# Pooled attention with expert routing: eleven unread TensorE products under the first loads, eighteen more behind the first bound sums and among the first maxima, and new places for the first three pairs

## The chip, the core and the metric

The kernel runs on one core of a Trainium2 chip. The core has TensorE (matmul), VectorE, ScalarE, GpSimd and SyncE (which issues most DMAs); each works through its own list of instructions in order and waits on semaphores for the others. The metric is the device time of one execution, in microseconds, as the median of several runs. Lower is better.

## The reference

The kernel computes attention with pooled queries, and then an expert layer with a fixed capacity on its output. Cut to what matters:

```python
def _attn_ref(q, k, v):                      # each (8, 8, 1152, 64)
    q_pool = q.reshape(B, H, S // 2, 2, D).mean(axis=3)
    scores = 1 / np.sqrt(D) * np.matmul(q_pool, k.transpose(0, 1, 3, 2))
    scores = scores - np.max(scores, axis=-1, keepdims=True)
    attn = np.exp(scores)
    attn = attn / (np.sum(attn, axis=-1, keepdims=True) + 1e-09)
    return np.matmul(attn, v)

def _moe_ref(x, w_gate, w1, w2):             # 4608 tokens, 8 experts, 576 each
    logits = x @ w_gate
    ...                                      # tokens to experts, best logit first, 576 per expert
    for e in range(E):
        out[mask_e] = np.maximum(x[mask_e] @ w1[e], 0) @ w2[e]
```

The change touches only the attention part, and there only how it begins.

## The kernel before, in words

Attention works on 32 pairs of heads. A pair takes 18 steps, nine blocks of 128 keys for each of its two heads `s`. A step is: scores on TensorE (`qk`, line 776, into `sc0` or `sc1`), the exponential on ScalarE (line 779, into `P`), the low half of the weights on GpSimd or VectorE (`PM`, line 783), and five steps later the weighted sums on TensorE (line 793, into `av0` or `av1`). Operands are split into a high and a low 16-bit half (`KH` and `KL`, `QH` and `QL`), so each score is a sum of products of 128 and of 65 or 69 rows.

Before a pair's steps come its preparations:

- Loads by SyncE: `QD` or `QS` (queries), `KD` (keys, two halves), `VD` (values), and `WB`, a piece of an expert's weights.
- Bounds (`bounds`, lines 520 to 581): ScalarE sums absolute values and squares into `VM` and `VQ`, TensorE adds them over the partitions into `mb` (tag `vs`, lines 537 to 545), VectorE takes the exponent bits into `VE` (lines 553, 555, 558), ScalarE makes the scales `SC` and `EX` (lines 564 to 573), VectorE the limit (line 576).
- Splits (`split`, `values`): `KH`, `QH`, scaled `KD` and `QS`, then `KL`, `QL`, and the two halves of the values in `V`. For the first two pairs GpSimd makes the low halves, later VectorE.
- `spread`: SyncE copies these halves to the tiles from which the scores are made (`KA`, `KB`, `QA`, `QB`).
- Row maxima (`max_chunk`): TensorE makes products of `QH` and `KH` and VectorE reduces each to a maximum. For pair 0 these are 15 chunks for head 0 (tags `mm0`, `mr0`) and 15 for head 1 (`mm1`, `mr1`), each a product of 64 rows by 384 columns (line 684, maxima at line 687); the chunks of head 0 use the five banks `ma`, `av0`, `sc0`, `av1`, `sc1`. For later pairs there are 18 chunks of 512 columns and three of the ends (lines 693 and 703, maxima at 696 and 705). A fold (line 724), a transpose into `mb` (line 738) and, for pair 0, two instructions with `ndiag` (lines 742 and 745) put the maxima into rows of `QB`; the scores of a head need them.

Pair 0's maxima, its splits and its copies therefore stand before the first score.

The order of all this is set ahead of time. `Cycle.plan` puts the items into a list by a number from a table: for an item of tag `x` the number is the table's entry plus 25 times its pair, and the smallest number whose inputs are already in the list comes next. Pairs 0, 1 and 2 have tables of their own, `TAU0`, `TAU1` and `TAU2`; all others use `TAU`. Each engine then runs its items in the list's order; waits on the chip follow from the tiles that they read and write.

Unread products (tags `wu`, `wv`, `wx`, line 916) multiply a tile of ones with a tile of ones, 128 rows by 512 columns, into `av0` or `av1`; nothing reads the result. There are 10 of tag `wu` and 13 of tag `wx`. The table puts five of them at the start, five behind pair 0's first bound sums, and 13 between the chunks of the maxima.

## Time and profile before

| | |
|---|---|
| median of 3 runs | 1232.99 us |
| lowest and highest | 1231.44 and 1235.9 us |
| profiled execution | 1237.53 us, of which its span 1235.8 us |
| TensorE busy | 1190.0 us, 96% of the span |
| VectorE, ScalarE, GpSimd busy | 82%, 79%, 73% |

The profile is of one execution, and all later rows are of it. A timeline row gives the start, the length and the engine of an instruction or of several alike, the line in the program, and in brackets how long the engine stood idle before it and what released it. A row of the chain of waits is one piece of the path that ended last. A row of the windows view gives the busy time of each engine in a stretch.

### The profile page before, as it was taken

The numbers are of one execution on the slowest core, as the hardware profiler recorded it, in microseconds if no ns is written. First come the engines' busy times: TensorE is split into PE (matmuls) and PEld (weight loads), VectorE is DVE, ScalarE is ACT, GpSimd is POOL, SyncE is SP. The second block draws the span as 40 slices with busy tenths as digits, with TensorE's granted clock in tenths as the row PEclk, the third lists the DMA queues.
The fourth block names the chain that finished last, engine by engine and source line by source line (L and its number), as shares of the span: only waits on it lengthen the run. The fifth ranks groups of instructions, "written<-read, shape, count | busy, mean of one in ns | idle before, by whom it ended". The sixth has DMA issues, their size and how long they took to land.

```text
span 1235.8 us, 38902 instructions
## 1 busy us (share of the span) xinstructions
PE 1190.0 (96%) x15470; PEld 860.7 (70%) x15470; DVE 1018.7 (82%) x2743; ACT 972.0 (79%) x1719; POOL 901.6 (73%) x879
## 2 busy tenths in 40 slices
PE   7899999999999999999999999789999999999998
PEld 2567778778778777777787788465657466575673
DVE  6899899999999999999999995779888898893520
ACT  6979899999899898999999986065876686786751
POOL 6978898898888998888888887044775584675641
PEclk9999999999999999999999999889999999999999
DMA  8666776876776866776876730042453554547401
GB/s 250 151 158 165 186 189 163 196 186 160 191 185 160 193 182 162 195 184 159 197 188 157 180 93 20 20 175 86 129 196 111 159 192 130 171 138 230 120 31 39
DMA packets 131218, 190.83 MB, mean 154 GB/s; under 512 B 50268, under 2 KB 86108, under 8 KB 128732
## 3 DMA queue, kind: packets, MB, share of 16 engines
q1 hardware_dynamic: 117948, 126.75, 38.9%
q0 software_dynamic: 12944, 61.58, 17.5%
q8 instruction: 121, 1.98, 0.7%
q14 instruction: 61, 0.50, 0.1%
q10 hardware_dynamic: 144, 0.02, 0.0%
HBM read 116.41 MB, written 18.87 MB: 109 GB/s over the span
## 4 chain that ended last, share of the span: by engine, by line
PE 77%; DVE 13%; DMA 4%; issue 2%; ACT 2%; POOL 0%; SPq 0%; POOLq 0%; ACTq 0%; DVEq 0%
PE sc L776 20%; PE av L793 18%; PE ph L1561 11%; PE po L1591 11%; PE mb L693 4%; PE ma L693 4%; DVE MX L696 3%; PE av L828 1%; DMA BD<-QH 1%; PE av L840 1%; ACT P L779 1%; DMA W<-in_w_dram,widx 1%; PE po L1597 1%; PE rt L1194 1%; DVE HX L1570 1%
## 5 line engine op out<-in xcount | busy, mean ns | idle before, releaser
L783 POOL TENSOR_TENSOR PM<-P 128x576 f16<-128x576 f32 x508 | 612.4, 1266 | 99.6 <-ACT P L779 48.3
L779 ACT ACTIVATE P<-sc,EX 128x576 f32<-128x576 f32 x576 | 412.6, 739 | 76.0 <-PE sc L776 58.8
L793 PEld LDWEIGHTS <-P 128*128 128x128 bf16 x5760 | 293.0, 98 | 30.0 <-issue 1.9
L793 PE MATMUL av<-V,P 128*128 128x65 f16 (+1 forms) x5760 | 301.2, 192 | 0.0
L793 PE MATMUL av<-V,PM 128*128 128x65 f16 x2880 | 292.8, 194 | 0.0
L793 PEld LDWEIGHTS <-PM 128*128 128x128 f16 x2880 | 263.8, 97 | 0.0
L776 PE MATMUL sc<-QA,KA 128*128 128x288 f16 x1152 | 234.5, 285 | 1.4 <-ACT P L779 1.3
L776 PE MATMUL sc<-QB,KB 65*128 65x288 f16 (+1 forms) x1152 | 235.7, 285 | 0.0
L696 DVE TENSOR_REDUCE MX<-mb 128x1 f32<-128x512 f32 x279 | 190.7, 684 | 27.8 <-PE mb L693 22.7
L696 DVE TENSOR_REDUCE MX<-ma 128x1 f32<-128x512 f32 x279 | 190.6, 683 | 9.8 <-PE ma L693 6.8
L776 PEld LDWEIGHTS <-KA 128*128 128x128 f16 x1152 | 106.2, 97 | 73.1 <-issue 22.7
L1591 PE MATMUL po<-W2H,HX 128*128 128x512 f16 x512 | 155.5, 379 | 0.0
L1561 PE MATMUL ph<-XH,W1H 128*128 128x320 f16 (+1 forms) x512 | 146.2, 286 | 0.7 <-DVE WE L1539 0.3
L1561 PE MATMUL ph<-XL,W1H 128*128 128x320 f16 (+1 forms) x512 | 146.2, 286 | 0.6 <-DVE XL L1455 0.6
L1561 PE MATMUL ph<-XH,W1L 128*128 128x320 f16 (+1 forms) x512 | 145.9, 286 | 0.0
L776 PEld LDWEIGHTS <-KB 65*128 65x128 f16 (+1 forms) x1152 | 112.5, 98 | 29.4
L1591 PEld LDWEIGHTS <-HX 128*128 128x128 f16 x768 | 71.2, 98 | 78.5 <-issue 0.5
L1561 PEld LDWEIGHTS <-W1H 128*128 128x128 f16 x1024 | 97.9, 98 | 30.7 <-issue 6.1
L1613 POOL DMA_INDIRECT out_dram<-OT,idx x40 | 39.2, 980 | 109.1 <-ACT OT L1593 91.2
L693 PE MATMUL ma<-KH,BD 128*128 128x512 f16 x279 | 105.7, 379 | 3.5 <-DVE MX L696 1.3
L693 PE MATMUL mb<-KH,BD 128*128 128x512 f16 x279 | 105.5, 378 | 3.3 <-DVE MX L696 1.4
L1514 POOL TENSOR_TENSOR W2L<-W,W2H 128x512 f16<-128x512 f32 x64 | 73.2, 1159 | 38.5 <-ACT W L1512 34.1
(308 smaller groups left out, 2157.9 us busy)
## 6 DMA issues: line engine op xcount, KB each, us to landing
KD<-in_kt_dram SPq DMA_DIRECT2D x64, 288.0 KB
VD<-in_v_dram SPq DMA_DIRECT2D x32, 576.0 KB
WB<-in_w_dram SPq DMA_DIRECT2D x32, 512.0 KB
QA<-QH SPq DMA_DIRECT2D x128, 72.0 KB
KB<-KH SPq DMA_DIRECT2D x64, 144.0 KB
KA<-KH SPq DMA_DIRECT2D x64, 144.0 KB
KA<-KL SPq DMA_DIRECT2D x64, 144.0 KB
x_dram<-X SPq DMA_DIRECT2D x16, 576.0 KB
```

Source lines behind the costliest of these rows:

```text
L693: od.add(t, "PE", 214, lambda: nc.tensor.matmul(m, BD[i][:, j, :], KH[i][:, 512 * c:512 * c + 512], start=True, stop=True), r=bd + [("KH", ...
L696: od.add(t, "DVE", 597, lambda: nc.vector.tensor_reduce(MX[i][:, j, c:c + 1], m, axis=AX.X, op=OP.max), r=[mk], w=[("MX", i, j, c)], tag=" ...
L776: nc.tensor.matmul(c[:, t, :288], a[i][:rows, s, ks], b[i][:rows, s, 288 * t:288 * t + 288], start=first, stop=not first)
L779: od.add(g + 0.1, "ACT", 624, lambda: nc.scalar.activation(p.rearrange("p (t q) -> p t q", t=2), c[:, :, :288], AF.Exp, scale=EX[n % 3][:, ...
L783: od.add(g + 0.2, en, dur, lock=1, fn=lambda: eng.tensor_tensor(pm, p, hi, op=OP.subtract), r=[("P32", g % NP)], w=[("PM", g % NM)], tag="pm")
L793: nc.tensor.matmul(out, w[:, qs], v, start=kb == 0 and j == 0 and y == 0, stop=kb == NKB - 1 and y == 2, skip_group_check=True)
L828: nc.tensor.transpose(m[:, 128 * z:128 * z + 128], X[u][:, 3 * q + z], ident)
L840: nc.tensor.matmul(av[1][32 * q:32 * q + E, :384], wgs[:, c], XT[q].rearrange("p c t -> p (c t)"), start=True, stop=True)
L1514: od.add(tt, "POOL", 1230, lambda o=lo[p], a=raw[p], h=hi[p]: nc.gpsimd.tensor_tensor(o, a, h, op=OP.subtract), r=[key, hk, sk], w=[(nm + ...
L1561: nc.tensor.matmul(p, a[:, d, fs], b[:, d, qs], start=z == 0, stop=z == 11)
L1591: nc.tensor.matmul(o, a[:, z, q0:q0 + 128], b[:, z], start=z == 0 and y == 0, stop=z == 7 and y == 2)
L1613: st = nc.gpsimd.indirect_dma_start(out=out, out_offset=bass.IndirectOffsetOnAxis(ap=idx[i][:n, c:c + 1], axis=0), in_=OT[ob][:n], in_offs ...
```

## The change

Three things are done.

1. Tables: eleven unread products (`wu`) now stand at the very start, and the 13 of tag `wx` are gone.
2. In `bounds`, for pair 0, a new item of tag `wv` runs six unread products into `av1` behind the first bound sums. In `max_chunk`, each chunk of head 0 but three is followed by one unread product into the second half of `sc0`. That makes 11 + 6 + 12 = 29 unread products where there were 23.
3. `TAU0`, `TAU1` and `TAU2` get new numbers throughout; `TAU`, and with it the order of the other 29 pairs within themselves, stays.

```diff
-... "wu": [-17.875, -17.555, -17.235, -16.915, -16.595, -16.275, -15.955, -15.635, -15.315, -14.995], "wx": [...]
+... "wu": [-300, -299.99, -299.98, -299.97, -299.96, -299.95, -299.94, -299.93, -299.92, -299.91, -299.9], "wv": [-250],
...
-      5, "np": 10, "nm": 10, "stick": 1, "nx": 3, "wu": 10, "pd": [4, 12], "wv": 0, "pd0": [], "pd1": [1, 2, 4, 9, 10,
-      15, 16, 17], "d1": 2.0, "cw1": 0.7, "wx": 13, "wy": 0}
+      5, "np": 10, "nm": 10, "stick": 1, "nx": 3, "wu": 11, "pd": [4, 12], "wv": 0, "pd0": [], "pd1": [1, 2, 4, 9, 10,
+      15, 16, 17], "d1": 2.0, "cw1": 0.7, "wx": 0, "wy": 0}
...
         od.add(t + AT["bs"], "DVE", 250 if not a else 190, bits, r=["mb"], w=[("VE", i, c) for c in range(a, b)], tag="vs")
+        if not n and not a:
+            def busy():
+                for _ in range(6):
+                    nc.tensor.matmul(av[1], ones, wide, start=True, stop=True)
+            od.add(t + AT["bs"], "PE", 1280, busy, r=["mb"], w=["av1"], tag="wv")
...
-            od.add(t, "PE", 163, lambda: nc.tensor.matmul(
-                m[:q, :384], QH[i][r, 128 * j:128 * j + q], KH[i][r, 384 * c:384 * c + 384], start=True, stop=True),
-                r=[("QH", i)] + [("KH", i, z) for z in ((0,), (0, 1), (1,))[c]], w=[mk], tag="mm" + "01"[h])
+
+            def chunk():
+                nc.tensor.matmul(m[:q, :384], QH[i][r, 128 * j:128 * j + q], KH[i][r, 384 * c:384 * c + 384], start=True, stop=True)
+                if not h and (j, c) not in ((0, 2), (2, 1), (2, 2)):
+                    nc.tensor.matmul(sc[0][:, 1], ones, wide, start=True, stop=True)
+
+            od.add(t, "PE", 163 if h else 376, chunk, r=[("QH", i)] + [("KH", i, z) for z in ((0,), (0, 1), (1,))[c]], w=[mk], tag="mm" + "01"[h])
```

How the lists move at the places that matter here. First TensorE, from pair 0's bound sums to the first products of the maxima (`down` and `VM` are of the bound sums, `ones` and `wide` of the unread products, `sc_166` is `sc0`, `av_169` is `av1`). Before:

```order
L542 MATMUL mb<-VM_126,down 128x2 [waits Activation_49]
L916 LDWEIGHTS ones
L916 MATMUL av_169<-wide,ones 128x512
...
L684 LDWEIGHTS QH_89 [waits DVE_49]
L684 MATMUL av_169<-KH_85,QH_89 128x384 [waits Activation_49]
L684 LDWEIGHTS QH_89
L684 MATMUL sc_166<-KH_85,QH_89 128x384
```

and after:

```order
L541 MATMUL mb<-VM_126,down 128x2 [waits Activation_49]
L565 LDWEIGHTS ones
L565 MATMUL av_169<-wide,ones 128x512
...
L690 LDWEIGHTS QH_89 [waits DVE_49]
L690 MATMUL sc_166<-KH_85,QH_89 128x384 [waits Activation_49]
L692 LDWEIGHTS ones
L692 MATMUL sc_166<-wide,ones 128x512
L690 LDWEIGHTS QH_89
L690 MATMUL av_169<-KH_85,QH_89 128x384
L692 LDWEIGHTS ones
L692 MATMUL sc_166<-wide,ones 128x512 [waits DVE_49]
```

Five unread products (now six) precede the first chunk in both; behind each chunk now stands one into `sc0`, and the second of these waits for VectorE, for the maximum that reads `sc0`'s first half (two more of the twelve wait in the same way).

Second ScalarE, from pair 0's scales to its splits (`SC_113`, `EX_116` are the scales, `VJ,VQ<-VD` is the square over the values). Before:

```order
L564 ACTIVATE SC_113<-VE_135 128x2
L572 ACTIVATE EX_116<-SC_113 128x1
L573 ACTIVATE EX_116<-VE_135 128x1
L595 ACTIVATE KH_85<-KD_119,SC_113 128x576
L600 ACTIVATE QS_124<-QS_124,SC_113 128x576
L595 ACTIVATE KH_85<-KD_119,SC_113 128x576
L598 ACTIVATE KD_119<-KD_119,SC_113 128x576
L532 ACTIVATE VJ,VQ<-VD_122 128x1152
```

and after:

```order
L568 ACTIVATE SC_113<-VE_135 128x2
L599 ACTIVATE KH_85<-KD_119,SC_113 128x576
L576 ACTIVATE EX_116<-SC_113 128x1
L577 ACTIVATE EX_116<-VE_135 128x1
L604 ACTIVATE QS_124<-QS_124,SC_113 128x576
L531 ACTIVATE VJ,VQ<-VD_122 128x1152
L599 ACTIVATE KH_85<-KD_119,SC_113 128x576
L602 ACTIVATE KD_119<-KD_119,SC_113 128x576 x2
```

KH's first half moves ahead of both EX, its second half behind the square over VD.

Third VectorE, where `ndiag` is built. Before, among the last maxima of head 0:

```order
L687 TENSOR_REDUCE MX_137<-ma 128x1
L687 TENSOR_REDUCE MX_137<-sc_166 128x1
L493 TENSOR_SCALAR ndiag<-scratch 128x640 [waits Pool_49]
L687 TENSOR_REDUCE MX_137<-sc_166 128x1 [waits PE_49]
L687 TENSOR_REDUCE MX_137<-ma 128x1
L724 TENSOR_REDUCE CM_106<-MX_137 128x4 [waits DVE_49]
```

and after, ahead of the first work on a loaded tile:

```order
L394 MEMSET floor 128x3
L395 MEMSET floor 128x1
L492 TENSOR_SCALAR ndiag<-scratch 128x640 [waits Pool_49]
L592 TENSOR_TENSOR QS_124<-QD_121 128x576 [waits DMAHW1_49]
L500 MEMSET P_140 128x64
```

It leaves the list of the maxima and stands under the first loads.

## Rows read from the trace of the kernel before

**Rows 1.** Windows: stretch, length, busy us of PE, PEld, DVE, ACT, POOL, then PEclk.

```profile
24.40:55.76 31.36, 28.22 (x393) 18.53 (x393) 24.75 (x55) 27.98 (x49) 28.90 (x25) 1.00 0.52 139
...
55.76:79.30 23.54, 20.38 (x265) 13.99 (x263) 21.47 (x43) 17.52 (x31) 17.35 (x19) 1.00 0.63 149
...
125.00:725.00 600.00, 597.70 (x9944) 474.56 (x9942) 554.21 (x1095) 550.24 (x954) 525.07 (x467) 1.00 0.71 177
```

**Rows 2.** Chain of waits: start us, length us, what.

```profile
38.50 4.35 DVE MX L696 x7
...
69.26 2.52 DMA QB<-QL
```

**Rows 3.** Timeline, TensorE: start us, us, line, out<-in, [idle before <-releaser].

```profile
3.34 2.30 PE L916 MATMUL av<-wide,ones 128*128 128x512 bf16 x5 [3.34 <-DVE floor L396]
...
8.88 2.29 PE L916 MATMUL av<-wide,ones 128*128 128x512 bf16 x5
...
11.10 0.50 PE L684 MATMUL av<-KH,QH 64*128 64x384 f16 x1
...
17.00 1.01 PE L916 MATMUL av<-wide,ones 128*128 128x512 bf16 x2
...
18.40 2.31 PE L916 MATMUL av<-wide,ones 128*128 128x512 bf16 x5
...
21.31 1.25 PE L916 MATMUL av<-wide,ones 128*128 128x512 bf16 x5
...
24.18 0.32 PE L684 MATMUL mb<-KH,QH 64*128 64x384 f16 x1 [0.77 <-DVE QB L745]
...
24.43 0.42 PE L776 MATMUL sc<-QA,KA 128*128 128x288 f16 x2
```

**Rows 4.** Timeline, opening: TensorE's first wait, then ScalarE.

```profile
8.05 0.16 PE L540 MATMUL mb<-VM,down 128*128 128x1 bf16 x1 [2.40 <-ACT VJ L528]
...
9.49 0.30 ACT L572 ACTIVATE EX<-SC 128x1 f32<-128x1 f32 x1
...
9.88 0.76 ACT L595 ACTIVATE KH<-KD,SC 128x576 f16<-128x576 f32 x1
...
12.54 1.15 ACT L532 ACTIVATE VJ<-VD 128x1152 bf16<-128x1152 f32 x1
```

**Rows 5.** Timeline, opening: VectorE.

```profile
11.64 0.56 DVE L687 TENSOR_REDUCE MX<-av 128x1 f32<-128x384 f32 x1 [1.32 <-PE av L684]
...
14.69 2.15 DVE L687 TENSOR_REDUCE MX<-av 128x1 f32<-128x384 f32 x4 [0.48 <-PE av L684]
...
18.50 0.55 DVE L687 TENSOR_REDUCE MX<-sc 64x1 f32<-64x384 f32 x1 [0.96 <-PE sc L684]
...
19.91 0.47 DVE L493 TENSOR_SCALAR ndiag<-scratch 128x640 f32<-128x640 int32 x1
...
21.42 0.56 DVE L687 TENSOR_REDUCE MX<-sc 128x1 f32<-128x384 f32 x1 [1.03 <-PE sc L684]
...
22.47 0.17 DVE L724 TENSOR_REDUCE CM<-MX 128x4 f32<-128x12 f32 x1
...
23.18 0.75 DVE L742 SCALAR_TENSOR_TENSOR QB<-mb,CB,ndiag 5x512 f16<-5x512 f32 x1 [0.48 <-PE mb L738]
```

**Rows 6.** Timeline: GpSimd, and SyncE's issue of KL.

```profile
13.42 2.85 POOL L603 TENSOR_TENSOR KL<-KD,KH 128x576 f16<-128x576 f32 x2
...
16.30 1.10 SPq L642 DMA_DIRECT2D KA<-KL  x2
...
25.95 7.78 POOL L783 TENSOR_TENSOR PM<-P 128x576 f16<-128x576 f32 x7 [3.26 <-ACT P L779]
```

**Rows 7.** Timeline, VectorE between pair 0 and pair 1.

```profile
55.52 0.82 DVE L670 SCALAR_TENSOR_TENSOR V<-VD,SC,V 128x576 f16<-128x576 f32 x1 [0.75 <-ACT V L667]
...
56.25 0.81 DVE L635 SCALAR_TENSOR_TENSOR KL<-KD,SC,KH 128x576 f16<-128x576 f32 x1
...
58.68 0.69 DVE L696 TENSOR_REDUCE MX<-mb 128x1 f32<-128x512 f32 x1 [0.56 <-PE mb L693]
```

More of the change, by code (lines that the diff above doesn't have):

```diff
@@ L272 @@
[L272 removed]
[5 rows of a table removed]
[L278 to L281 removed]
[7 rows of a table removed]
[L289 removed]
[4 rows of a table removed]
[L294 removed]
+TAU0 = {"abk": [-3.247596, -6.270317], "abs": [-22.78447, -0.5571336], "aug": [-49.20042, -63.65756], "augt":
[5 rows of a table added]
+        [-101.5423, -18.87479, -31.42721, -95.43, 4.982884, -83.49272, -8.005609, -143.5481, 16.64426], "expb":
+        [-22.75529, -40.03387, -77.62868, -79.1448, -30.53657, -2.177917, -18.52933, -29.97288, -77.77242],
+        "fill": [17.15927, -27.82857, -23.76563, -16.43919, -137.43, -18.75261, -69.09106, 10.14575, 16.42628,
[12 rows of a table added]
+        0.8312891, -116.2708, -51.32051, -17.92582, 24.11002], "qkb": [-41.59464, -18.72518, -6.461611,
[7 rows of a table added]
@@ new lines @@
+TAU2 = {"abs": [-23.4975, -25.08641, -26.23569], "aug": [-14.60879], "augd": [-37.69011, -17.43024], "augt":
[5 rows of a table added]
+        [-51.9563, -87.83583, 11.56729, 11.74051, 4.501346, 17.61292, 8.607434, -26.29048, -67.10155], "expb":
+        [4.700961, -115.0573, -24.42258, 11.60432, 13.4284, -4.90717, 4.748511, -105.6011, -6.529959], "fold":
+        [-9.159572], "kh": [-31.96585, -24.85616], "kl": [-132.7912, -32.1933], "ld": [-27.96813, -84.05359],
+        "ldq": [-139.8815], "ldv": [-53.46438], "ldw": [-78.02513], "me": [-15.49425, -10.66331, -2.929244],
[7 rows of a table added]
+        [3.485547, 5.850303, 7.472656, -68.70809, 16.64328, 17.42214, 19.19644, 21.93961, 27.13442], "qkb":
[4 rows of a table added]
+        -116.044], "vsh": [-45.67116], "wsq": [10.11431], "x": [34.10587, -12.73376]}
```

42 lines of the change are left out of this document (12 added, 30 removed), and 99 rows, old and new, of tables (TAU0, TAU1, TAU2).

## The prediction

> **What bounds the kernel now.** I read the windows view first, to see which engine is full where. From 125 to 725 us the TensorE row is busy 597.70 of 600 us, VectorE 554.21 [rows 1]: there TensorE sets the pace, and the end moves with whatever moves the start of that stretch. The order of those pairs isn't touched. So the change can only be worth what it does in the opening: the wait until the first scores at 24.43 us [rows 3], and the idle of TensorE while the first pairs run, 31.36 - 28.22 = 3.1 us from 24.40 to 55.76 and 23.54 - 20.38 = 3.2 us from 55.76 to 79.30 [rows 1]. Second, the chain of waits: between the first scores and pair 1's it runs over VectorE's row maxima (4.35 us in one piece at 38.50) [rows 2]. VectorE's list of maxima thus carries an earlier start on, if it starts earlier itself. Third, the timelines of the opening, engine by engine [rows 3 to 5].
>
> In the opening two things are to be seen. The unread products run 512 columns in 0.43 us (five in 2.31 us at 18.40), which is 1.2 GHz, and only the five at 21.31 take 1.25 us together, which is 2.4 GHz [rows 3]; the granted clock in the windows reads 1.00 throughout there, so I go by the pitch of the rows. And the first head's 15 maxima on VectorE run from 11.64 to 22.47 with three waits for TensorE of 0.48, 0.96 and 1.03 us and the building of ndiag at 19.91 among them [rows 5]: 2.47 us of waits and about 0.5 us of other work in a chain that sets the first scores.
>
> **The change, part by part.** *Products under the first loads.* Eleven stand where five stood: 11 x 0.43 = 4.7 us from 3.34 to 8.0. The next product that must wait for something does so until 8.05 (ScalarE's sum) [rows 3, 4], so they cost nothing; if the loads came sooner, they would cost up to 6 x 0.43 = 2.6 us. Six more follow the bound sums at 8.88, one more than before: 2.6 us at the low clock (to 11.4), 1.3 us at the high one (to 10.2).
>
> *When the clock rises.* Before, it rose between 18.40 and 21.31: seven full-height products (two from 17.00, five from 18.40) with a product of the maxima between stood ahead of it. The five from 8.88 did not raise it; what followed them at once, from 11.10, were products of 64 rows [rows 3]. Now eleven full ones run without a gap and six more follow 0.8 us later, so I expect 2.4 GHz at about 8 to 10 us. Nothing in the trace shows this order itself; the bounds are "at once" and "as late as before".
>
> *ScalarE.* The first half of KH moves ahead of the two small EX instructions: it began at 9.88, 0.39 after the first of them at 9.49, and would begin at 9.49 and end at 10.25 [rows 4]. The square over VD moves ahead of KH's second half, so that half ends near 13.1 instead of 12.0 (such a square took 1.15 us at 12.54 [rows 4]). KD follows it, so KL on GpSimd starts near 13.9 instead of 13.42 and, at 2.85 us for both, ends near 16.8 [rows 6].
>
> *VectorE.* With the first product at 10.3 and VectorE's EX and CB behind ScalarE's EX, the first maximum starts at about 10.9 instead of 11.64: 0.7 us. Ndiag moves under the first loads, where VectorE waits for QD anyway: 0.5 us. The 15 maxima go on at 0.52 us each (the chain's 1.03 for two, of the row 21.42), 7.7 us, plus 0.35 for the value bound. The three waits (2.47 us) go at the high clock, since a product and its companion need 0.16 + 0.21 us. New waits come: a companion writes the second half of sc0, and three of the twelve wait for a maximum that reads its first half (the DVE waits in the order), about 0.15 to 0.2 us each on VectorE, and the third maximum of the first round waits on one too; I count 0.7 us in four places. So the fold starts at 10.9 + 7.7 + 0.35 + 0.7 = 19.65 instead of 22.47. One maximum of the second head now stands between the fold and the QB rows, 0.3 us of which isn't covered by the transpose: QB from 20.65 instead of 23.18 [rows 5]. **First scores at 21.85 instead of 24.43: 2.5 us.**
>
> *What comes next there.* ScalarE: squares and splits for pair 1 now stand in one row to about 21.7, 0.6 us before the first exponential can start; covered. GpSimd: two BD clears, an iota, a transfer and both V parts follow KL, some 6.5 us, to 23.3; the first PM can't start before 23.2. Before, GpSimd waited 3.26 us at this place [rows 6]; that cover is used up, and what it is late beyond 23.3 goes through its 7 PM in a row (7.78 us). KL's transfer is issued near 16.8 instead of 16.30 [rows 6]; the trace shows no landing of it, only the first scores at 24.43 as the latest. The nearest seen transfer took 2.52 us, at 69.26 [rows 2]. So KL lands 2.5 to 8.1 us after its issue, at 19.3 to 24.9; I take a value under 21.8, since the scores came late for another reason (QB), which the timeline shows.
>
> *Pairs 0 to 2.* The remaining 14 maxima of the second head and the 22 of pair 1 keep their order but for a place or two; VectorE carries 2.5 us on to pair 1. There one order matters: both KL now stand ahead of the V part. Before, V waited until 55.52 and the second KL began only at 56.25; the next maximum started at 58.68 after a wait of 0.56 [rows 7]. With the KL back to back the row up to the sums' division ends 0.7 us sooner, if V is ready in time (one KH later on ScalarE), so 0 to 0.7; I take 0.4. The other moves in TAU1 and TAU2 I bound by the idle that they could close or open, a third of 6.3 us: plus or minus 2, taken as nought.
>
> **Sum**: 0.7 + 0.5 + 2.47 - 0.7 - 0.3 is 2.7, of which the times above keep 2.5; plus 0.4: 3 us earlier. The profiled execution took 1237.5 us (span 1235.8); it would take 1234.5. The median of the runs is 1233.0; 1233.0 - 3.0 = **1230.0 us**.
>
> **Rivals.** (a) *The clock rises late*, at 13 to 14 us, in the first round of maxima. Then the six fillers end at 11.4, the first maximum starts at 12.4, and 1.5 us of the 2.6 are lost: 1231.7. For it: before, the five full products of 8.88 and the maxima products right behind them did not do it. Against: those behind were of 64 rows, and now seventeen full ones stand there [rows 3]. (b) *The clock isn't released in the opening*: the slower side. From 11.4 at 1.2 GHz, 15 products x 0.32 + 12 companions x 0.43 = 10 us, plus 1.5 us of waits for maxima that share sc0, ends at 22.9; last maximum 23.7, fold, transpose and QB 1.8: first scores at 25.7, 1.3 us later than before, and half-rate scores after it some 0.5: 1234.8. It decides if the rise comes after about 19 us. (c) *The clock falls again.* After the rise TensorE has 0.37 us of work per 0.52 us maximum, with pauses of up to 1.4 us at the companions that wait. Before, after 21.31, it waited 0.77 us until 24.18 and the scores at 24.43 still ran fast (two products of 288 columns in 0.42) [rows 3], which speaks against. At the low clock the second round would be bound by products: 10 x 0.32 + 7 x 0.43 = 6.2 us instead of 5.2, and the transpose and first scores add 0.5: 1231.5. The Trainium skill, page "TensorE: Matmul & The Clock Gate", section "A second HAM failure mode: psum-queue depth-cycling", describes this: small pauses between groups of products, while PSUM banks are cycled, can make the clock swing between its levels. By that page the sum would be this rival's; the trace speaks for the other so far. (d) *KL's transfer gates*: landing at 24.9 as the far bound gives nothing, 1233.4; a landing of 22.8 gives 1231. (e) *The new orders of pairs 1 and 2 close more of the idle*, 1 to 3 us of the 6.3: 1227 to 1229. The counterpart, waits that they open, gives 1232 to 1236.
>
> **How the numbers follow.** About 0.3% (3.7 us) is what a measurement of this kernel can tell from no change. Forecast (2 to 3.7 us gained) 0.43; (e) 0.22, of which a little stays under 3.7 us; its counterpart 0.08, half of it over 3.7 us slower; (a) 0.10; (b) 0.06; (c) 0.05; (d) 0.06. Only (e) is over 3.7 us faster, and the upper end of the forecast with the scatter of the runs (1231.4 to 1235.9) adds to it: faster 0.31. Slower by over 3.7 us: half the counterpart and a part of (b): 0.07. The rest, 0.62, is within. The range leaves out the far end of (e) and most of (b) and the counterpart: 1226.6 to 1234.3.
>
> **What would show it.** In the profile after: the second group of fillers under 1.6 us for six (clock up by 10) or 2.6 us (rival a); the first maximum at 10.9; the fold at 19.7; ndiag before 5.6; first scores near 21.9, with GpSimd's first PM near 23.3; pair 1's first scores near 53.2; and TensorE full from about 97. If the first scores stand at 22 but the later pairs don't follow, a wait of GpSimd or a transfer in pair 0 took it. Wrong would be a first score after 24.4, or a gain of over 4 us that starts in pairs 1 and 2.

## The result and the profile after

The changed kernel takes 1244.32 us (median of 6 runs, 1241.8 to 1247.98) against 1233.62 us (6 runs, 1231.44 to 1237.23): 1.0092 of the kernel before, 95% interval 1.0074 to 1.0109, some 11 us slower. Forecast were 1230.0 us and at most 1234.3.

The windows view first, in the stretches of [rows 1] and in shorter ones (stretch, length, busy us and instructions of PE, PEld, DVE, ACT, POOL, then PEclk, DMA share, GB/s):

```profile
24.40:55.76 31.36, 28.89 (x230) 15.10 (x230) 20.46 (x42) 20.82 (x34) 23.14 (x21) 0.72 0.38 100
55.76:79.30 23.54, 19.29 (x278) 13.57 (x277) 18.45 (x42) 19.61 (x38) 17.19 (x18) 1.00 0.61 155
125.00:725.00 600.00, 597.63 (x9968) 474.52 (x9966) 554.16 (x1097) 550.16 (x954) 524.88 (x469) 1.00 0.72 177
...
16.00:20.00 4.00, 3.21 (x10) 0.78 (x8) 3.18 (x7) 3.97 (x7) 3.64 (x8) 0.77 1.06 191
20.00:24.00 4.00, 2.92 (x7) 0.75 (x8) 2.56 (x8) 1.85 (x5) 2.43 (x2) 0.50 1.08 209
...
40.00:44.00 4.00, 3.32 (x58) 2.50 (x56) 2.12 (x7) 3.25 (x5) 3.41 (x3) 0.74 0.24 58
44.00:48.00 4.00, 3.69 (x22) 2.14 (x23) 3.50 (x7) 2.59 (x4) 3.98 (x5) 1.00 0.86 212
```

Full pace from 125 to 725 us is as before, 597.63 of 600 us. The difference stands in the first line: a granted clock of 0.72 from 24.40 to 55.76 us, where before had 1.00 [rows 1], and 230 products done there instead of 393. The shorter stretches say when: it falls within 16 to 20 us, is 0.50 (1.2 GHz) from 20 on, and rises within 40 to 44. TensorE's timeline shows the same by the pace of its products (start, length, line, and in brackets the idle time before and what ended it):

```profile
2.10 4.85 PE L924 MATMUL av<-wide,ones 128*128 128x512 bf16 x11 [2.10 <-DVE wide L390]
...
8.58 2.72 PE L565 MATMUL av<-wide,ones 128*128 128x512 bf16 x6
11.24 0.36 PE L690 MATMUL sc<-KH,QH 64*128 64x384 f16 x1
11.53 0.39 PE L692 MATMUL sc<-wide,ones 128*128 128x512 bf16 x1
...
12.57 0.38 PE L692 MATMUL sc<-wide,ones 128*128 128x512 bf16 x1 [0.38 <-DVE MX L695]
...
17.15 0.38 PE L692 MATMUL sc<-wide,ones 128*128 128x512 bf16 x1 [0.80 <-DVE MX L695]
...
18.41 0.61 PE L692 MATMUL sc<-wide,ones 128*128 128x512 bf16 x1
...
25.24 0.66 PE L784 MATMUL sc<-QA,KA 128*128 128x288 f16 x2
...
40.44 0.29 PE L801 MATMUL av<-V,P 128*128 128x65 f16 x2
...
44.37 0.41 PE L784 MATMUL sc<-QA,KA 128*128 128x288 f16 x2
...
64.02 0.41 PE L784 MATMUL sc<-QA,KA 128*128 128x288 f16 x2 [0.78 <-DMA QA<-QH]
```

An unread product takes 0.39 us when it runs alone at 2.4 GHz and 0.61 at 1.2. The clock is up from the first chunk (11.24) to about 18.2, falls between the rows 17.15 and 18.41, and comes back among the weighted sums that begin at 40.44. The first scores stand at 25.24 us (before 24.43 [rows 3]) and run at half rate: two products of 288 columns take 0.66 us instead of 0.42. Pair 1's first scores are at 64.02; before, they stood here:

```profile
55.60 0.41 PE L776 MATMUL sc<-QA,KA 128*128 128x288 f16 x2
```

So pair 0 takes 38.8 us instead of 31.2, and pair 1 begins 8.4 us later. Behind it the distance changes little: pair 2 begins at 92.61 (83.48 before), 9.1 us apart, and the same scores of pair 5 stand at 164.93 (156.18), 8.8 apart. The first exponential of the last pair comes 9.7 us later. The profiled executions then end 7.1 us apart (spans of 1242.9 and 1235.8), because what follows that exponential takes 482.3 us here and 484.8 in the kernel before; in a second trace of the kernel before (e5 below) it takes 480.0, so this part varies by more than the difference. Most of the loss thus arises before 64 us.

The mean granted clock of the six executions is 0.982 to 0.984, that of the executions of the kernel before in the runs below with the same pace 0.990 to 0.998. From 18.2 to 42.1 us at half clock is 0.5 x 23.9 / 1243 = 0.010. A low stretch of about this length is thus in every execution of the changed kernel, not only in the profiled one.

### The profile page after: what moved, and what is told of

Its sections match the earlier page's. It is cut to its first block, busy times and chain, and to the rows that moved or that the text cites. A ratio compares the mean times of both kernels' runs of the same rounds, so it can differ in the third digit from the quotient of the medians.

```text
span 1242.9 us, 38914 instructions
## 1 busy us (share of the span) xinstructions
PE 1198.8 (96%) x15476; PEld 863.5 (69%) x15476; DVE 1019.0 (82%) x2743; ACT 971.8 (78%) x1719; POOL 902.1 (73%) x879
## 4 chain that ended last, share of the span: by engine, by line
PE 72%; DVE 12%; DMA 7%; issue 3%; ACT 3%; POOL 2%; SPq 1%; POOLq 0%; ACTq 0%; DVEq 0%
PE sc L784 19%; PE av L801 16%; PE ph L1569 11%; PE po L1599 10%; PE mb L701 4%; PE ma L701 4%; DVE MX L704 2%; DMA W<-in_w_dram,widx 2%; DMA BD<-QH 1%; PE av L836 1%; DMA QB<-AU 1%; POOL PM L791 1%; PE av L848 1%; DVE V L674 1%; PE rt L1202 1%
## 5 line engine op out<-in xcount | busy, mean ns | idle before, releaser
L784 PE MATMUL sc<-QB,KB 65*128 65x288 f16 (+1 forms) x1152 | 238.2, 288 | 0.2 <-DMA QB<-AU 0.2
L1522 POOL TENSOR_TENSOR W2L<-W,W2H 128x512 f16<-128x512 f32 x64 | 73.2, 1159 | 38.4 <-ACT W L1520 33.9
```

The lines of the kernel that those rows point to most:

```text
L784: nc.tensor.matmul(c[:, t, :288], a[i][:rows, s, ks], b[i][:rows, s, 288 * t:288 * t + 288], start=first, stop=not first)
L1522: od.add(tt, "POOL", 1230, lambda o=lo[p], a=raw[p], h=hi[p]: nc.gpsimd.tensor_tensor(o, a, h, op=OP.subtract), r=[key, hk, sk], w=[(nm + ...
```

## Experiments

Theory 1: the clock, which falls in the maxima and stays low through pair 0, is the loss. Theory 2: the new numbers of the three tables are. Each run is set against runs of the kernel before on the same chip, as a ratio, since the pace is not always the same: the kernel before takes 1257 us beside e1 to e4, 1259 beside e17 and e18, and 1233 beside the others. Times of a trace are one execution's. In the table the unread products are given as: at the start, behind the bound sums, among the first head's chunks, among the second head's. "Low until" is when the clock rises first; of the stretches in which it is low again those up to 83 us are given (e2, e4, e6 and e7, four of the nine traces with all three new tables, have one more of 3.4 us between 83 and 92 us).

| run | tables | unread products | ratio (95%) | pair 0's first scores | pair 1's | low until; low again |
|---|---|---|---|---|---|---|
| before | old | 5, 5, 13, 0 | 1 | 24.43 | 55.60 | 21.2 |
| after | new | 11, 6, 12, 0 | 1.0092 (1.0074-1.0109) | 25.24 | 64.02 | 11.3; 18.2-42.1 |
| e1 | old | 5, 5, 0, 0 | 1.0026 (1.0011-1.0041) | 22.44 | 60.84 | 41.1 |
| e2 | new | 5, 5, 13, 0 | 1.0038 (1.0022-1.0055) | 24.63 | 59.63 | 11.4; 14.8-21.7, 31.9-38.7 |
| e3 | old | 11, 6, 12, 0 | 1.0077 (1.0053-1.0101) | 23.40 | 61.66 | 7.4; 21.0-41.5 |
| e4 | new | 11, 6, 24, 0 | 1.0106 (1.0079-1.0134) | 24.45 | 63.04 | 5.4; 22.5-43.0 |
| e5 | old | 5, 5, 13, 0 | one run | 23.77 | 54.95 | 20.6 |
| e6 | new | 11, 6, 20, 0 | 1.0096 (1.0075-1.0118) | 26.12 | 64.17 | 6.3; 16.6-23.4, 26.8-43.9 |
| e7 | new | 5, 5, 0, 0 | 1.0046 (1.0025-1.0068) | 21.03 | 61.13 | 40.6 |
| e8 | old | 5, 5, 9, 0 | 1.0024 (1.0000-1.0047) | 22.90 | 62.73 | 46.1 |
| e9 | new | 5, 5, 13, 15 | 1.0053 (1.0033-1.0073) | 25.19 | 60.24 | 11.9; 15.3-22.1 |
| e10 | old | 5, 5, 13, 15 | 1.0034 (1.0022-1.0046) | 22.45 | 56.41 | 11.4; 14.8-18.3 |
| e11 | old | 5, 5, 9, 15 | 1.0032 (1.0009-1.0055) | 23.61 | 67.90 | 47.4 |
| e12 | new | 5, 5, 8, 15 | 1.0065 (1.0039-1.0092) | 24.29 | 68.74 | 47.3 |
| e13 | new | 11, 6, 12 in own banks, 0 | 1.0071 (1.0047-1.0096) | 21.10 | 59.91 | 7.3; 20.9-38.0 |
| e14 | old | 11, 6, 13, 0 | 1.0002 (0.9980-1.0024) | 22.73 | 53.91 | 6.5; 13.3-20.1 |
| e15 | new for pair 0 | 5, 5, 13, 0 | 1.0183 (1.0154-1.0211) | 24.25 | 75.18 | 20.8; 27.6-51.5 |
| e16 | new for 1 and 2 | 5, 5, 13, 0 | 1.0280 (1.0253-1.0308) | 23.73 | 84.03 | 20.8; 37.9-68.6, 75.4-82.2 |
| e17 | new | 11, 6, 16 (own banks), 6 | 1.0017 (1.0002-1.0032) | 21.07 | 54.74 | 5.9 |
| e18 | old | 11, 6, 17 (own banks), 4 | 1.0020 (1.0003-1.0037) | 24.53 | 57.06 | 6.1; 16.3-23.2, 33.4-36.8 |

### Products and tables taken apart: e1 to e4

e1, the kernel before without the 13:

```diff
-      ... "d1": 2.0, "cw1": 0.7, "wx": 13, "wy": 0}
+      ... "d1": 2.0, "cw1": 0.7, "wx": 0, "wy": 0}
```

> The kernel before with the 13 unread products between the chunks of the first head's maxima left out (tag wx), all else as it was. Theory 1, the clock: those products, 16.5 to 22.6 us in the rows of before, raise TensorE from 1.2 to 2.4 GHz at about 21 us, and without them the pace of the low clock (0.50 us shown for a 64-row product of 384 columns, 0.66 to 0.69 for a pair of score products) goes on into pair 0, as it did in the changed kernel until 42 us. Then the first scores come at about 22.5 to 24, pair 1's first scores some 6 to 9 us after those of before (55.8), and the median is 1239 to 1244 us. Theory 2, the tables: the unread products are of little weight and the loss of the changed kernel is in the new numbers for pairs 0 to 2. Then this run stands within 2 us of the kernel before, 1231 to 1236 us.

First scores at 22.44, at the low clock, which goes on to 41.1 us; pair 1's 38.4 us later. The 13 products cost 1.3 to 2 us before the first scores (23.77 and 24.43 in the two traces with them) and save 7 us behind them. Median 1260.93 against 1257.11 us, 1.0026. The mechanism is theory 1's; the size, 3.8 us, is under its 5 to 10, since the earlier first scores give a part back.

e2, the changed kernel with the products of the kernel before (5 and 5 for 11 and 6; a counter of the chunks sets the 13):

```diff
+                    for _ in range({12: 3, 13: 5, 15: 5}.get(chunks, 0)):
+                        nc.tensor.matmul(a free bank, ones, wide, start=True, stop=True)
-                if not h and (j, c) not in ((0, 2), (2, 1), (2, 2)):
-                    nc.tensor.matmul(sc[0][:, 1], ones, wide, start=True, stop=True)
```

> The changed kernel with its new tables, but with the unread products at the places that they had before: 5 at the start, 5 behind the bound sums, 3 after the 12th chunk of the first head, 5 after the 13th and 5 after the 15th, none elsewhere. Theory 1, the clock: it rises at about 20 to 21 us and stays up, the first scores come between 22.5 and 24.5 us, and the median is 1228 to 1234 us, at or a little under the kernel before (1233.6). Theory 2, the tables: the new order of the first three pairs costs about 10 us whatever the clock does, and the median is 1240 to 1246 us with pair 1's first scores after 60 us.

1.0038, between the two theories. In its trace the ten early products were enough to raise the clock at 11.4; it fell in the sparse maxima at 14.8, the 13 raised it at 21.7, and it fell once more among pair 0's scores at 31.9.

e3, the old three tables in the changed kernel (its products stay):

```diff
-TAU0, TAU1, TAU2 = (the new numbers)
+TAU0, TAU1, TAU2 = (the old numbers, with the new entries "wu" and "wv")
```

> The kernel before with its old tables, but with the unread products of the changed kernel: eleven at the start, six behind the bound sums, one behind twelve chunks of the first head. Theory 1, the clock: it rises at about 11 us, falls again at about 18 us as in the changed kernel, and stays low till the first weighted sums at about 40 us; median 1240 to 1246 us. Theory 2, the tables: the old order keeps its time, or gains the 1 to 2 us of an early clock: 1230 to 1235 us.

1.0077: most of the change's loss, without its tables. TensorE's timeline of e3 about the fall and at the first scores:

```profile
18.08 0.39 PE L692 MATMUL sc<-wide,ones 128*128 128x512 bf16 x1
19.25 0.32 PE L690 MATMUL ma<-KH,QH 64*128 64x384 f16 x1 [0.78 <-DVE MX L695]
19.71 0.32 PE L690 MATMUL sc<-KH,QH 64*128 64x384 f16 x1
21.49 0.45 PE L746 MATMUL mb<-ident,CM 128*69 128x128 f32 x1 [1.46 <-DVE CM L733]
21.88 0.50 PE L690 MATMUL ma<-KH,QH 64*128 64x384 f16 x1
22.99 0.48 PE L690 MATMUL mb<-KH,QH 64*128 64x384 f16 x1 [0.61 <-DVE QB L753]
23.40 0.66 PE L784 MATMUL sc<-QA,KA 128*128 128x288 f16 x2
```

From 18.5 to 21.5 TensorE does two products and waits 0.78 and 1.46 us for VectorE; a 64-row product takes 0.32 us before this and 0.50 after it. Pair 0 takes 38.3 us. Theory 1.

e4, two companions behind each chunk:

```diff
-                    nc.tensor.matmul(sc[0][:, 1], ones, wide, start=True, stop=True)
+                    for _ in range(2):
+                        nc.tensor.matmul(sc[0][:, 1], ones, wide, start=True, stop=True)
```

> The changed kernel with two unread products behind each of the twelve chunks instead of one. At the high clock a chunk with two takes 0.16 + 2 x 0.21 = 0.59 us, over the 0.46 us of VectorE's maximum by 0.13. Theory 1, the clock: TensorE pauses less, the clock that rose at about 11 us stays up through the maxima, the first scores come at 22 to 23.5 us, 2.5 us or less after the forecast of one companion, and the median is 1229 to 1234 us; if two still don't hold it, the clock falls later than 18 us and the time stays over 1238. Theory 2, the tables: twelve more products make it later by 1 to 2 us than the changed kernel, 1245 to 1247 us.

The clock held longer, to 22.5 us, but the second companion slowed the maxima and the clock fell in the pauses before the first scores: 1.0106. The first theory's number did not come; its condition (the clock stays up) was not met. 1.0106 is also what the second theory named (1245 to 1247 us are 1.009 to 1.011), so this run does not part the two.

### Does the old kernel keep its clock, and what do the tables cost: e5 to e8

e5 is the kernel before, unchanged.

> The kernel before, unchanged, for a second trace of it. Theory 1, the clock: the 13 unread products from 16.5 to 22.6 us raise TensorE to 2.4 GHz in every execution, so the first scores at about 24 us run at 0.42 us for two products of 288 columns, no granted clock of 0.5 stands between 24 and 700 us, and pair 1's first scores come 31 to 33 us after pair 0's. The rival: the rise at 21 us in the first trace was that execution's luck; then this one shows 0.66 us for the same products, and pair 1's first scores 37 to 39 us after pair 0's.

The second trace repeats the first: rise at 20.6, no fall before 774 us, pair 1's first scores 31.2 us behind pair 0's.

e6, eight more products behind the 15th chunk of the changed kernel:

```diff
+                if chunks == 15:
+                    for _ in range(8):
+                        nc.tensor.matmul(a free bank, ones, wide, start=True, stop=True)
```

> The changed kernel with eight more unread products behind the 15th chunk of the first head, where VectorE's last maxima, the fold and the transpose are waited for; all else of it stays. At the low clock they take 8 x 0.43 = 3.4 us, of which about 1.3 us lie in waits that are there now. Theory 1, the clock: it is at 2.4 GHz again by 26 us instead of 42, the scores of pair 0 run at full speed, pair 1's first scores come 31 to 34 us after pair 0's instead of 38.8, and although the first scores are 1 to 2 us later the median is 3 to 6 us better than the changed kernel, 1.003 to 1.007 of the kernel before. Theory 2, the tables: the additional products only delay, 1.010 to 1.012.

1.0096, a miss: they did raise the clock (23.4), but it fell again at 26.8 among pair 0's first scores. By the ratio this is close to theory 2's number, by the trace it is the clock again: it was low through most of pair 0, until 43.9.

e7, the new tables with ten products only (no companions, 5 for 11 and 5 for 6):

```diff
-                if not h and (j, c) not in ((0, 2), (2, 1), (2, 2)):
-                    nc.tensor.matmul(sc[0][:, 1], ones, wide, start=True, stop=True)
```

> The new tables with only the ten unread products 5 at the start and 5 behind the bound sums, none among the maxima: the same products as in the run with the old tables and without the 13 (which stood at 1.0026 of the kernel before). The two differ in the tables alone. Theory 1, the clock alone decides: also 1.001 to 1.005, first scores at 20.5 to 23 us, pair 1's first scores 37 to 39 us behind them. Theory 2, the tables cost something by themselves: 1.006 or more, with pairs 1 and 2 longer than the 27.9 and 25.1 us from first scores to first scores of the run with the old tables.

First scores at 21.03, 1.4 us before e1's: what the new order of the opening is worth at the low clock. Pair 1's at 61.13, 0.3 us behind e1's; pair 2's at 91.18 and 88.72. 1.0046 against e1's 1.0026, with intervals that overlap and on different chips: theory 1 for most, and a cost of the new order behind the first scores.

e8, nine of the 13:

```diff
-      ... "wx": 13, "wy": 0}
+      ... "wx": 9, "wy": 0}
```

> The kernel before with nine instead of 13 unread products among the maxima of the first head: 1 and 1 about the value bound's sums, 3 instead of 5 behind the 13th chunk, 4 instead of 5 behind the 15th. Theory 1, the clock with a price: without the 13 the first scores came 2 us earlier but at half rate, so the products cost about 0.15 us each in the opening and give 7 us in pair 0. With nine the first scores come 0.6 to 1 us earlier, 23.4 to 23.8 us, and if the clock still rises by about 24 us the ratio is 0.998 to 1.000. If nine are too few to raise it, pair 0 takes 38 us to pair 1's first scores and the ratio is 1.002 to 1.005.

Its twelve times spread from 1229.19 to 1244.73 us. The traced one (1243.66) had the low clock to 46.1 us. The fast end, below the fastest run of the kernel before (1231.54), fits an execution in which nine were enough; no trace shows one, and the twelve times form no two clear groups. The 13 are not a luxury: in all eight traces that have them (before, e2, e5, e9, e10, e14, e15, e16) the clock is up from 18.3 to 22.1 us on, in the three with eight or nine (e8, e11, e12) only from 46 to 47 us, in the two with none (e1, e7) from 41.

### Holding the clock among pair 0's scores: e9 to e12

Each adds one unread product behind each of the second head's 15 chunks (in e9 and e12 into whichever bank is free); e9 to e2, e10 to the kernel before, e11 to e8, and e12 (1, 3 and 4 behind the 12th, 13th and 15th chunk) to e7:

```diff
+                if h:
+                    nc.tensor.matmul(av[1], ones, wide, start=True, stop=True)
```

> The new tables with the unread products of the kernel before (5, 5, and 3, 5, 5 behind the 12th, 13th and 15th chunk) and one more behind each of the 15 chunks of the second head, which run among pair 0's scores. Theory 1, the clock: it rises at 18 to 24 us and these hold it up through pair 0 (in the run without them it fell at 31.9 us); pair 1's first scores come 31 to 33 us after pair 0's, and the ratio to the kernel before is 0.997 to 1.002. Theory 2, the tables cost by themselves: no granted clock of 0.5 in pair 0, and still 1.003 or more, with pair 1 over 28.6 us long.

> The kernel before with one unread product behind each of the 15 chunks of the second head. At the high clock each takes 0.21 us, 3.2 us in all, against 3.1 us of idle in that stretch. If the kernel before keeps its clock in every execution (two traces of it do), they are only a cost: ratio 1.000 to 1.002. If it loses the clock in pair 0 in some executions, its scatter (1231.5 to 1238.2) shrinks and the ratio is 0.998 to 1.000. Either way this is the partner with the old tables of the run with the new tables and the same products; the difference of the two is what the tables are worth at the high clock: nought to 1 us better by theory 1, 4 us or more worse by theory 2.

> The old tables with nine unread products among the first head's maxima and one behind each of the 15 chunks of the second head. With nine alone the time fell in two groups, 1229 to 1234 us where the clock rose before the first scores and 1236 to 1245 us where it rose with the weighted sums. Theory 1, the clock: the products among the scores raise it by about 30 us where the nine did not, so the slower group disappears; median 1230 to 1235 us, ratio 0.997 to 1.001. If they don't raise it, they only lengthen the low stretch, by up to 15 x 0.43 = 6.5 us: 1.004 to 1.009.

> The new tables with 5 and 5 unread products, then 1, 3 and 4 behind the 12th, 13th and 15th chunk of the first head, and one behind each of the 15 chunks of the second head. With no products among the maxima the new tables had their first scores at 21.03 us, 1.4 us before the old tables. If the clock is up by 25 us here (theory 1), first scores at 22.5 to 23.5 us, pair 1's 31 to 33 us later, ratio 0.996 to 1.000: the gain of about 3 us that the prediction worked out. If not, pair 0 takes 38 to 41 us and the ratio is 1.003 to 1.008.

e9 and e10 have the clock up from 22 and 18 us to 776 and more. Pair 0 takes 35.1 and 34.0 us; with the old tables that is 2.8 more than without these products (31.2), which don't fit into the idle (1.0034 where at most 1.002 was expected). Pairs 1 and 2 take 28.6 and 25.6 us with the new tables, 27.9 and 25.1 with the old, and e9's ratio is 1.0053: over 1.003 with the clock up, as theory 2 has it, but 0.0034 of it are the products'. At the high clock the new tables are thus no gain, and by these traces a loss of 2 us over three pairs; the two ratios' intervals overlap. The traces of e11 and e12 have no rise before 47 us, and there the additional products lengthened the low stretch, to 44 us for pair 0; e11's twelve times still spread from 1230.8 to 1245.9.

### Why the clock falls: e13 and e14

e13, each companion ahead of its chunk and in the chunk's own bank:

```diff
+                if not h and (j, c) not in ((0, 2), (2, 1), (2, 2)):
+                    nc.tensor.matmul(m, ones, wide, start=True, stop=True)
                 nc.tensor.matmul(m[:q, :384], QH[i][r, ...], KH[i][r, ...], start=True, stop=True)
-                if not h and (j, c) not in ((0, 2), (2, 1), (2, 2)):
-                    nc.tensor.matmul(sc[0][:, 1], ones, wide, start=True, stop=True)
```

> The changed kernel with each of the twelve companions put ahead of its chunk and into the chunk's own bank, so that none writes sc0 beside a maximum that reads it. Theory A, the waits: TensorE's pauses of 0.38, 0.80 and 0.20 us for the maxima of sc0 let the clock fall at 18 us; without them it holds to the first scores, which come at 22 to 23.5 us, and the ratio to the kernel before is 0.998 to 1.003. Theory B, one product per chunk is too little whichever bank it writes: the clock falls again between 14 and 22 us and stays at 0.5 until about 40 us, ratio 1.006 to 1.011.

TensorE's timeline of e13 behind the maxima:

```profile
16.98 0.33 PE L692 MATMUL ma<-KH,QH 64*128 64x384 f16 x1
18.25 0.32 PE L692 MATMUL ma<-KH,QH 64*128 64x384 f16 x1 [0.94 <-DVE MX L695]
18.60 0.30 PE L746 MATMUL mb<-ident,CM 128*69 128x128 f32 x1
19.22 0.32 PE L692 MATMUL ma<-KH,QH 64*128 64x384 f16 x1 [0.32 <-DVE MX L695]
20.20 0.32 PE L692 MATMUL mb<-KH,QH 64*128 64x384 f16 x1 [0.66 <-DVE QB L753]
21.10 0.64 PE L784 MATMUL sc<-QA,KA 128*128 128x288 f16 x2 [0.58 <-DMA KA<-KL]
```

The pauses inside the maxima are gone, the clock holds through them, and the first scores come at 21.10, 4 us before the changed kernel's. Before them TensorE waits 0.94, 0.32, 0.66 and 0.58 us, and the clock falls at 20.9, the moment the scores begin. This is theory A on the maxima, and it may be the same mechanism one stage later; the ratio, 1.0071, is theory B's.

e14, the old tables with the early products of the change and the 13 late ones of before:

```diff
-      ... "wu": [-17.875, -17.555, ...], "wx": [...]
+      ... "wu": [-300, -299.99, ..., -299.9], "wv": [-250], "wx": [...]
...
-      ... "wu": 10, ... "wx": 13, "wy": 0}
+      ... "wu": 11, ... "wx": 13, "wy": 0}
...
+                for _ in range(6):
+                    nc.tensor.matmul(av[1], ones, wide, start=True, stop=True)
```

> The old tables with the early products of the change, 11 at the start and 6 behind the bound sums, and with the 13 of the kernel before among the maxima; no companions. Theory A, the 13 decide: the clock may rise and fall early, but it is up from 24 us at the latest and stays; pair 1's first scores 31 to 33 us after pair 0's; ratio 0.997 to 1.002. Theory B, an early rise is itself the harm: the clock is low in pair 0 in some or all executions, ratio 1.004 or more.

1.0002: the clock rose at 6.5, fell in the maxima at 13.3, and the 13 had it up again at 20.1, with this timeline up to the first scores:

```profile
16.61 2.32 PE L934 MATMUL av<-wide,ones 128*128 128x512 bf16 x5
19.61 1.48 PE L934 MATMUL av<-wide,ones 128*128 128x512 bf16 x5
22.48 0.32 PE L692 MATMUL mb<-KH,QH 64*128 64x384 f16 x1 [0.77 <-DVE QB L763]
22.73 0.42 PE L794 MATMUL sc<-QA,KA 128*128 128x288 f16 x2
```

Over twelve executions the early rise does neither harm nor good beyond 0.2%; pair 0 takes 31.2 us as before. With e3, which has the same tables and the same early products, this shows what the change lost: the 13 products, which end in a dense run just before the first scores.

### The tables one by one: e15 and e16

```diff
 e15:
-TAU1, TAU2 = (the new numbers), in e2
+TAU1, TAU2 = (the old numbers)
 e16:
-TAU1, TAU2 = (the old numbers), in the kernel before
+TAU1, TAU2 = (the new numbers)
```

> The new table of pair 0 alone (TAU1 and TAU2 old), with the unread products at the places of the kernel before, as in the run with all new tables and these products (1.0038). If the new order of pair 0 is what costs there: 1.002 to 1.005, with the clock low in a part of pair 0 or pair 1's first scores over 32 us behind pair 0's. If it is TAU1 and TAU2: 0.997 to 1.001.

> The kernel before with the new tables of pairs 1 and 2 alone. Traces with the new tables took 28.6 to 30.4 us from pair 1's first scores to pair 2's and 25.6 to 27.5 us to pair 3's, those with the old ones 27.9 to 29.0 and 25.1 to 26.5, and four of the six with the new tables show a granted clock of 0.5 for 3.4 us at 83 to 92 us. If that is the order's doing, it shows here too and the ratio is 1.001 to 1.003; if not, 0.998 to 1.000.

1.0183 and 1.0280, outside of all that was expected. Pair 0 alone takes 51 and 60 us, with the clock low for 24 and 31 us of it. One pair's numbers are made for the order of its neighbours, and mixed they make waits that neither kernel has: in e15 ScalarE's list has sums over newly loaded KD and VD ahead of pair 0's first exponential and waits 6.00 us for the load of VD, so that this exponential starts 10.9 us behind the first scores, where it was 0.7 before. For e16 the waits were not followed. The two runs say nothing on which table the remaining loss is in.

### The pauses filled: e17 and e18

e17 adds to e13 four products behind the 15th chunk and 1, 3 and 2 behind the second head's first three chunks, that is, in the pauses just shown. e18 does the like with the old tables:

```diff
+                seen[h] += 1
+                for _ in range(({15: 4}, {1: 1, 2: 3, 3: 2})[h].get(seen[h], 0)):
+                    nc.tensor.matmul(av[1], ones, wide, start=True, stop=True)
```

> The changed kernel with the companions in their chunks' own banks (first scores at 21.1 us in that run, but the clock fell at 20.9) and ten more unread products in the pauses that were left there: 4 behind the 15th chunk, then 1, 3 and 2 behind the second head's first three chunks, 0.21 us each at the high clock. If the clock needs TensorE to have work up to the first scores and no more, it stays up, the first scores come at 21 to 22 us, pair 1's 31 to 33 us later, and the ratio to the kernel before is 0.996 to 0.999: the 2.5 to 3 us of the forecast. If the new order of pair 0 is itself too thin to hold it (it fell at 31.9 and at 26.8 us in two runs with the new table), the clock falls between 24 and 35 us and the ratio is 1.003 to 1.009.

> The old tables with the early products (11 and 6), a companion in the chunk's own bank ahead of twelve chunks, five unread products behind the 15th chunk as before, and 3 and 1 behind the second head's first two chunks. The old order of pair 0 never lost the clock in a trace once it was up. If the companions hold it through the maxima, VectorE sets the pace there: first scores at 21.5 to 22.8 us instead of 23.8 to 24.4, pair 1's 31 to 32 us later, ratio 0.998 to 0.9995. If the clock falls in the maxima all the same, the five behind the 15th chunk alone have to raise it again: first scores after 23 us and a ratio of 1.001 to 1.006.

The traced execution of e17 is the forecast's case: the clock is up from 5.9 to 780 us and the first scores stand at 21.07. First its TensorE timeline at the first scores, then TensorE's waits from 20 to 56 us (who waited for what, us in total, times, longest):

```profile
19.61 0.82 PE L697 MATMUL av<-wide,ones 128*128 128x512 bf16 x3
20.36 0.33 PE L694 MATMUL mb<-KH,QH 64*128 64x384 f16 x1
20.63 0.61 PE L697 MATMUL av<-wide,ones 128*128 128x512 bf16 x2
21.07 0.41 PE L789 MATMUL sc<-QA,KA 128*128 128x288 f16 x2
```

```profile
PE sc L789 <- DMA QA<-QH: 2.3, 1, 2.3
PE mb L706 <- DVE QB L758: 0.8, 1, 0.8
PE ma L694 <- DVE MX L700: 0.7, 1, 0.7
```

And yet pair 1 begins at 54.74 us, where the two traces of the kernel before have 54.95 and 55.60. Of the 2.7 to 3.4 us gained at the first scores 2.5 are gone by then, 2.3 of them in one wait for pair 1's queries. SyncE's timeline and the chain of waits of e17 show what it waited for:

```profile
43.58 0.33 SPq L518 DMA_DIRECT2D VD<-in_v_dram  x1
43.96 0.46 SPq L646 DMA_DIRECT2D KB<-KH  x1
44.46 0.60 SPq L646 DMA_DIRECT2D QA<-QH  x1
45.10 0.59 SPq L646 DMA_DIRECT2D QB<-QL  x1
45.74 0.60 SPq L454 DMA_DIRECT2D WB<-in_w_dram  x1
46.39 0.49 SPq L646 DMA_DIRECT2D QA<-QH  x1
```

```profile
46.39 8.22 DMA QA<-QH
```

In the new order the last copy of QA is issued behind the load of VD (576 KB), which waits for GpSimd's V part, and right behind WB (512 KB); it lands 8.22 us later. The changed kernel has the same queue ten us later (the copy issued at 56.26, 7.63 us, TensorE 0.78 us idle for it). Before, VD was issued at 46.51, this copy at 49.34, no WB between, and it is nowhere on the chain of waits, of which [rows 2] are two pieces. In five traces with the new tables (the changed kernel, e2, e9, e13, e17) the copy takes 7.56 to 8.22 us and TensorE waits 0.73 to 2.34 us for it; in no trace with the old tables does pair 1's start wait for a copy. In the changed kernel, too, the chain of waits from 40.59 us to pair 1's start runs not over VectorE's maxima but over GpSimd (PM, KL, QL and V), the load of VD and this copy. That the loads ahead of it hold the copy up is read from the order alone; no run moved them.

Over twelve runs e17 is 1.0017 (1253.2 us, the traced one, is the fastest; the others take 1258 to 1265). Their mean clocks, 0.983 to 0.989 against 0.993 in the traced one, lie where those of the kernel before beside them lie (0.984 to 0.992), so in how many of them the clock held is not shown. e18's trace lost the clock at 16.3, in the maxima, and again at 33.4, among the scores of pair 0: 1.0020. Ahead of the two falls its timeline has these rows:

```profile
15.11 0.38 PE L692 MATMUL av<-wide,ones 128*128 128x512 bf16 x1 [0.65 <-DVE MX L699]
31.13 0.32 PE L693 MATMUL ma<-KH,QH 64*128 64x384 f16 x1 [0.49 <-DVE MX L699]
```

The second fall also ends what was expected of the old order, that it keeps the clock through pair 0 once it is up. Neither run beats the kernel before.

## Why the prediction was wrong

**The clock, first half: right that it rises early.** It was to rise at 8 to 10 us; it rose at 11.3 in the profiled execution (near rival a's case: six products in 2.72 us, first maximum at 11.96), and at 5.4 to 7.4 in those of e3, e4, e6 and e13 with the same early products.

**The clock, second half: the step that failed.** The sum took it that what has risen stays. Rival (c) said that it may fall, had 0.05, and was priced at 1.5 us, over the second round of the maxima alone; rival (b) put "half-rate scores after it some 0.5". Measured is a clock at half until the weighted sums of pair 0, and 7.6 us for that stage (38.8 instead of 31.2 us). With the old tables, where the order does not change, the low clock alone costs 7.1 to 7.2 us there (38.4 in e1, 38.3 in e3). In the changed kernel a part of the 7.6 belongs to the new order instead: e17's traced execution takes 33.7 us at a full clock. In the chain of waits four score products took 1.07 us at the low clock where they took 0.60 in the kernel before, and nine of pair 0's 18 steps lie in the low stretch. First a piece of the chain after, then of the one before:

```profile
25.31 1.07 PE sc L784 x4
24.49 0.60 PE sc L776 x4
```

The Trainium skill's page "TensorE: Matmul & The Clock Gate", section "A second HAM failure mode: psum-queue depth-cycling", which the prediction weighed and set aside, was the better guide: frequent small idles of TensorE between groups of products, while PSUM banks are cycled, make the clock swing. The traces agree as far as they go: pauses of 0.38 and 0.80 us stand ahead of the fall in the changed kernel, of 0.78 and 1.46 in e3, of 0.65 and 0.49 in e18, and e17's traced execution, where those ahead of the first scores were filled, has no fall. They do not show that a pause alone does it: the kernel before waits 0.77 and 0.82 us at 24.18 and 36.77, e17 0.65 and 0.83 at 26.15 and 33.29, and the clock stays up. What I had read as evidence against a fall, the pause at 24.18 [rows 3], stood right behind a dense run of products, not behind 7 us of sparse ones. Why one pause is followed by a fall and another is not stays open.

**The 13 products.** I priced their removal as a gain (waits of 2.47 us that go). They are that, 1.3 to 2 us (e1), and they were also what carried the clock into pair 0, 7 us. The cover was named nowhere in the sum: I costed what the new products add, not what the old ones did.

**Companions in sc0: about the size, while the clock was up.** They were put at 0.7 us. At the high clock VectorE waited 0.27, 0.63 and 0.27 us, and the 0.63 is there with own banks too (e13). The fold came at 22.71 instead of 19.65 mostly for other terms of the sum: the first maximum started at 11.96, 1.1 us later than said, and behind the fall VectorE waited another 0.42, 0.42 and 0.65 us. With own banks the fold came at 18.23 (e13), with the same products in sc0 at 21.51 (e6); of these 3.3 us 0.7 are a later first maximum, and e6 had the low clock from 16.6 on, so they are not sc0's alone.

**The rest of the opening: right.** Ndiag stood at 4.14 us, VectorE's maxima run at 0.46 us each (said: 0.52), GpSimd ended its V parts at 22.6, and in e17 its first PM was at 22.58 (said: 23.3). With the companions' waits gone the first scores were at 21.1, 0.75 us before the forecast. KL's copy, rival (d), is what ended last there: in e13 it was issued at 15.71 and TensorE waited 0.58 us for it until 21.10. Two sums of the rivals are 0.2 us off (rival a gives 1231.5, rival b first scores at 25.5); the forecast does not rest on them.

**"VectorE carries 2.5 us on to pair 1": wrong.** At a full clock (e17) it was a copy in SyncE's queue that set pair 1's start, with the 2.3 us wait for QA. The prediction followed VectorE's list there and did not go through SyncE's; only its list of signs named a transfer in pair 0 as a place where the gain could go. The 0.4 us for KL ahead of V did not show either: both KL now run together at 61.50 us, and the next maximum waits 1.52 us for TensorE at 66.47.

**Pairs 1 and 2: taken as nought.** At the full clock pair 1 takes 28.6 us and pair 2 25.6 in the traces with the new tables (the changed kernel, e9, e12, e13, e17), 27.9 and 25.1 in those with the old ones: 1.2 us the wrong way, of which 0.2 to 1.0 are left at pair 4. This is the counterpart of rival (e), and inside its bound of 2.

**What stays open.** The new products alone, on the old tables, cost 0.77% (e3); the whole change costs 0.92%. The new tables with the old products cost 0.38% (e2), in part by the clock (31.9 to 38.7 us). How much of it is the queue of SyncE alone was not tried.

## What to carry to other kernels

A filler product is worth what the clock does for the work behind it, so price its removal by the next stage at half rate, not by the slot it frees. In this kernel a run of 13 that reaches up to the first scores was worth 7 us, and the products spread thinly over a stage that waits for another engine raised the clock and lost it again. A dense run is no guarantee: behind the eight of e6 the clock fell again after 3.4 us, with the first scores just begun. So look at the clock in more than one trace. And when a stage starts earlier, read every queue that feeds the next one, the DMA issue queue too.

## What the runs showed of the hardware

The same ten products (5 and 5) raised the clock at 11.4 to 11.9 us in three traces (e2, e9, e10) and not in the nine others that begin with them, though the order of the work up to there is the same in e10 and the kernel before, and in e2 and e7. All eight traces with 11 and 6 have the rise at 5.4 to 11.3 us. One trace of an opening is one draw; with nine late products the twelve times of one kernel spread over 15.5 us (e8), and those of the kernel before beside it over 6.7.

In the changed kernel TensorE is busy 4.00 of 4 us from 28 to 32, with products of 64, 69 and 128 rows mixed, at a granted clock of 0.50 (1.2 GHz). The clock rises only at 42.1, 1.6 us into the weighted sums, all of 128 rows.

```profile
28.00:32.00 4.00, 4.00 (x16) 1.76 (x15) 1.58 (x3) 2.15 (x3) 2.96 (x4) 0.50 0.00 0
```

The granted clock reads 1.00 until the first change that the trace holds: in e1 it reads 1.00 throughout to 41 us while two products of 288 columns take 0.66 us. Ahead of the first rise only the pace of the products tells the level.
